# Cosine attention into a gated MLP on one core: scores in threes over three PSUM banks, norms by batch statistics and Newton steps, the last tile in three pieces

## The chip, the cores and the metric

The kernel runs on one core of a Trainium2 chip. The metric is the device time of one execution in microseconds (us); the times of before are the median of 4 runs. TensorE is called PE here, VectorE DVE, ScalarE ACT, GpSimd POOL, and SyncE SP, as in the profile.

## What is computed

8 batches, 12 heads, 448 positions, 64 elements a head, in float32; then an MLP from 768 to 2048 and back.

```python
q_n = q / (np.linalg.norm(q, axis=-1, keepdims=True) + 1e-06)
k_n = k / (np.linalg.norm(k, axis=-1, keepdims=True) + 1e-06)
scores = np.matmul(q_n, k_n.transpose(0, 1, 3, 2)) / tau
scores = scores - np.max(scores, axis=-1, keepdims=True)
attn = np.exp(scores)
attn = attn / (np.sum(attn, axis=-1, keepdims=True) + 1e-09)
x = np.matmul(attn, v)          # (B, H, S, D) -> (B * S, H * D)
h = x @ w_in
g = h * np.cos(h)
out = g @ w_out
```

## The kernel before

**Stages.** The work is cut into 48 pairs of heads (g = 0 to 47, six to a batch, PB = 6) and 16 units of three pairs (u, UP = 3). A unit is loaded in float32 (`load`, line 647 on, q and k; `load_v`), and normed: `square` (L689 on ACT, L691 on DVE, L693 on POOL), `reduce` (L700, DVE: a sum over 64 elements), `rnorm` (L708 and L711, ACT: ln, then exp of -0.5 ln, which is 1/norm), and `scale` (L719, DVE or POOL), which writes q and k as bf16 into `qks`. `transposes` (L734 by DMA from pair BYPE = 9 on, L745 on PE before) makes `qkT`. `scores` (L762) are four chunks a pair, each two matmuls on 64 rows that run side by side, into one of two banks SC0 and SC1; L767 is the exp that reads a chunk and writes PX. `attend` (L785) multiplies PX by v in the AV bank, L794 and L795 divide by the sum that a column of ones gave, and the result goes to xT by DMA (L801) or, for the pairs in XPE, by PE through the AV bank (L809, called XP) and a DVE copy (L813).

When a batch's six pairs are there, `m1` (L826) multiplies by w_in in eight groups over the banks AV, SC0 and SC1 in turn; L840 is ACT's cosine, L842 DVE's product, written to gT. ACT loads a table ahead of the cosines and another behind them (L618). `m2_emit` (L877) multiplies gT by w_out: a tile of 128 rows in two halves of 384 columns, 16 matmuls each, in the banks PO and PO2; DVE copies a half (L884) and SP sends the tile (L895), the last tile half by half (L891, SP and ACT).

**Order.** A planner sets it. Each operation has an engine, its reads and writes, a cost and a latest time; `play` places operations one by one, `arrange` tries several margins and keeps the plan whose rehearsal is shortest, and `emit` writes each engine's instructions in the order of the plan, with the semaphore waits that the reads and writes need. So every engine's order is fixed in the program. PE's operations come in two streams: A (scores, attend, M1, transposes) in groups of which the first three are looked at, and B (M2), of which only the first that is left is looked at (`fill[0]`) when A has nothing that is ready in time. In the first batch (`free`) the order of A is looser. Where PE would stand still in the head, `emit` puts in fillers, products of zeros (line 919, tile zt).

Loads of q, k, v go out on SP (the q of unit 0 on ACT), the weights on POOL with a cast to bf16: w_in in two halves (W1, L908), w_out in four (W2, L914). W1's first half waits until v of unit 0 has landed. A unit has its buffer by its number's last bit, so unit 2 is loaded into unit 0's, pair by pair, once unit 0's scales have read it.

**The steady part.** `pair(g)` gives the order: two chunks of scores, attend of the pair before, then two chunks. Between those PE does M2 of the batch before. After the first pair of a batch comes M1 of the batch before.

The functions that the diff touches:

## Time and profile before

| | |
|---|---|
| median of 4 runs | 433.74 us (433.16 to 434.6) |
| profiled execution | 432.82 us |
| its span, first to last instruction | 430.9 us |
| granted TensorE clock | 1.000 |
| PE busy | 417.8 us (97%), 13.7 of it fillers |
| ACT, DVE, POOL busy | 264.5, 212.9, 192.7 us |
| M1 of the first batch starts | 36.40 us |
| last matmul's row, start and length | 424.77, 2.76 us |

The page's second part shows the span in 40 slices, each digit the busy share in tenths. Groups of instructions are told by line, engine, operation, out<-in with shapes, count, busy time, mean, and the idle time just before them with what ended it. A timeline has the start, the length, engine, line and tiles of instructions in order, like ones merged with their count; in square brackets stands the idle time before one and what released it. PE's matmuls are pipelined: the distance of two starts tells what PE spends, the mean length is longer.

### The profile page before, as it was taken

What the parts mean: (1) busy time and instruction counts of PE and PEld (TensorE: products, weight loads), DVE (VectorE), ACT (ScalarE), POOL (GpSimd) and SP (SyncE); (2) the same over time, 40 slices, a digit from 0 to 9 for tenths busy, and PEclk for the clock granted to TensorE, in tenths of its full rate; (3) what the DMA queues carried; (4) which work ended last, traced back from release to release, by engine and by line L of the source; (5) the groups of instructions that cost most, each with busy time, mean ns of one, the idle gap of its engine ahead of it and who ended that gap; (6) DMA issues with size and microseconds to landing.
All of it is one profiled execution on the core that took longest, in us unless ns stands there. A gap on an engine that the chain in (4) does not pass through costs nothing.

```text
span 430.9 us, 8767 instructions
## 1 busy us (share of the span) xinstructions
PE 417.8 (97%) x3756; PEld 225.8 (52%) x3756; DVE 212.9 (49%) x297; ACT 264.5 (61%) x319; POOL 192.7 (45%) x118
## 2 busy tenths in 40 slices
PE   7889989999999999999999999999999999999996
PEld 2455545545555555555555545555555545555663
DVE  5776646464636366524853375425853343344221
ACT  3887386974777647874677638774777547734000
POOL 3995167923776556922496057913496000000000
PEclk9999999999999999999999999999999999999999
DMA  8999999898189596649757692649447102200322
GB/s 235 262 242 215 240 261 175 143 263 192 34 193 237 112 278 164 124 102 237 185 113 122 166 275 58 113 128 265 127 110 131 49 0 59 59 2 2 102 79 77
DMA packets 94631, 63.87 MB, mean 148 GB/s; under 512 B 55040, under 2 KB 89600, under 8 KB 94592
## 3 DMA queue, kind: packets, MB, share of 16 engines
q1 hardware_dynamic: 90064, 56.16, 55.3%
q0 software_dynamic: 3680, 6.29, 7.9%
q10 hardware_dynamic: 848, 0.86, 0.7%
q8 instruction: 30, 0.49, 0.5%
q14 instruction: 9, 0.07, 0.1%
HBM read 45.61 MB, written 11.01 MB: 131 GB/s over the span
## 4 chain that ended last, share of the span: by engine, by line
PE 83%; ACT 6%; issue 4%; DMA 3%; POOL 2%; DVE 2%; SPq 0%; POOLq 0%; ACTq 0%
PE PO L877 31%; PE SC L826 16%; PE AV L785 11%; PE AV L826 10%; PE SC L762 10%; ACT PX L767 5%; DMA raw<-in_q_dram 3%; PE SC L877 2%; POOL sq L693 1%; PE AV L877 1%; PE AV L809 1%; DVE gT L842 1%; PE PO L745 0%; POOL va L667 0%; DVE n L700 0%
## 5 line engine op out<-in xcount | busy, mean ns | idle before, releaser
L767 ACT ACTIVATE PX<-SC 112x896 bf16<-112x896 f32 x192 | 165.0, 914 | 43.8 <-PE SC L762 43.3
L877 PE MATMUL PO<-W,gT 128*128 128x384 bf16 x816 | 148.6, 326 | 0.0
L693 POOL TENSOR_TENSOR sq<-raw 112x1024 bf16<-112x1024 f32 x42 | 79.3, 1905 | 98.5 <-DMA raw<-in_q_dram 95.1
L877 PEld LDWEIGHTS PO<-W,gT 128*128 128x128 bf16 x816 | 73.0, 97 | 56.8 <-issue 13.1
L719 POOL TENSOR_TENSOR qks<-raw,rn 112x1024 bf16<-112x1024 f32 x47 | 88.4, 1902 | 29.6 <-ACT rn L711 29.4
L826 PE MATMUL SC<-xT,W 128*128 128x448 bf16 x480 | 95.5, 352 | 0.4 <-ACT PX L767 0.4
L842 DVE TENSOR_TENSOR gT<-SC,cosb 128x896 bf16<-128x896 f32 x40 | 43.5, 1091 | 55.1 <-ACT cosb L840 54.8
L840 ACT ACTIVATE cosb<-SC,cst 128x896 f32<-128x896 f32 x40 | 40.2, 1007 | 48.6 <-PE SC L826 46.1
L826 PEld LDWEIGHTS SC<-xT,W 128*128 128x128 bf16 x480 | 46.6, 98 | 43.2 <-issue 0.8
L700 DVE TENSOR_REDUCE n<-sq 112x16 f32<-112x1024 bf16 (+1 forms) x49 | 58.1, 1192 | 14.0 <-POOL sq L693 9.3
L826 PE MATMUL AV<-xT,W 128*128 128x448 bf16 x288 | 58.7, 352 | 1.1 <-DVE gT L842 0.5
L762 PE MATMUL SC<-qkT 64*128 64x448 bf16 x384 | 55.4, 355 | 4.4 <-ACT PX L767 2.2
L785 PEld LDWEIGHTS AV<-va,PX 112*128 112x128 bf16 x1536 | 49.4, 97 | 15.7 <-issue 11.3
L785 PE MATMUL AV<-va,PX 112*128 112x65 bf16 x1536 | 54.8, 193 | 1.1 <-ACT PX L767 1.1
L884 DVE COPY osb<-PO 128x384 f32<-128x384 f32 x51 | 28.2, 553 | 39.0 <-PE PO L877 39.0
L840 ACT ACTIVATE cosb<-AV,cst 128x896 f32<-128x896 f32 x24 | 24.2, 1007 | 32.6 <-PE AV L826 32.5
L794 DVE RECIPROCAL rcp<-AV 112x8 f32<-112x8 f32 x48 | 10.0, 207 | 66.9 <-PE AV L785 66.9
L826 PEld LDWEIGHTS AV<-xT,W 128*128 128x128 bf16 x288 | 27.5, 98 | 28.8 <-issue 3.9
L842 DVE TENSOR_TENSOR gT<-AV,cosb 128x896 bf16<-128x896 f32 x24 | 26.2, 1090 | 18.7 <-ACT cosb L840 18.6
L795 DVE TENSOR_TENSOR xs<-AV,rcp 112x512 bf16<-112x512 f32 x48 | 33.2, 692 | 2.0
L762 PEld LDWEIGHTS SC<-qkT 64*128 64x128 bf16 x384 | 13.2, 93 | 36.9 <-ACT PX L767 17.4
L667 POOL CAST va<-vin 112x1536 bf16<-112x1536 f32 x14 | 20.5, 1465 | 9.1 <-DMA vin<-in_v_dram 6.2
(34 smaller groups left out, 122.0 us busy)
## 6 DMA issues: line engine op xcount, KB each, us to landing
vin<-in_v_dram SPq DMA_DIRECT2D x16, 672.0 KB, 9.9
raw<-in_k_dram SPq DMA_DIRECT2D x12, 672.0 KB, 8.1
raw<-in_q_dram SPq DMA_DIRECT2D x12, 672.0 KB, 10.1
W<-in_moe_w_in_dram POOLq DMA_DIRECT2D x2, 1536.0 KB, 14.6
W<-in_moe_w_out_dram POOLq DMA_DIRECT2D x4, 768.0 KB, 21.3
raw<-in_k_dram SPq DMA_DIRECT2D x12, 224.0 KB, 6.9
out_dram<-osb SPq DMA_DIRECT2D x7, 336.0 KB, 2.8
out_dram<-osb SPq DMA_DIRECT2D x8, 288.0 KB, 2.7
```

Source lines behind the costliest of these rows:

```text
L693: pool(lambda e, x=x, y=y: e.tensor_tensor(y, x, x, ALU.mult), src_, dst, 0.1 + n * 1.78e-3, label="sq%d.%d" % (u, p))
L700: dve(lambda e, w=w: e.tensor_reduce(out=n2v[i][:, 2 * p : 2 * p + 2, w], in_=sqv[p][:, :, w, :], axis=mybir.AxisListType.X, op=ALU.add), ...
L719: f = lambda e, s0=s0, s1=s1: e.tensor_tensor(qksv[i][:, p, s0:s1, :, :].rearrange("p s h d -> p h s d"), rawv[i][:, h, s0:s1, :], bass.AP ...
L762: t = e.matmul(SCv[z][:, a, 0:S], qkT[k].ap()[r, NP * c : NP * c + 128], qkT[k].ap()[r, S : 2 * S], start=True, stop=True)
L767: act(lambda e: e.activation(PXv[j][:, c, 0 : 2 * S].rearrange("p (a s) -> p a s", a=2), SCv[z][0:NP, :, 0:S], ACT.Exp, scale=1.0 / TAU), ...
L785: t = e.matmul(AVv[:, a, DV * x : DV * x + n], PXv[j][:, c, k : k + 128], vav[i][:, NJ * (2 * p + a) + c, 0:n], start=(c == 0), stop=(c == ...
L795: dve(lambda e: e.tensor_tensor(xsv[y].rearrange("p x h d -> p h x d"), AXv[:, :, :, 0:D], bass.AP(rcp[y], 0, [[NS, NP], [NJ, 2], [1, NJ], ...
L826: t = e.matmul(ph[:, a, 0:S], W1v[:, c, 128 * n : 128 * n + 128], xTv[b % 2][:, c, :], start=(c == 0), stop=(c == NKC - 1))
L840: act(lambda e, ph=ph, cz=cz: e.activation(cosv[cz], ph[:, :, 0:S], ACT.Sin, bias=cst.ap()[:, 0:1], scale=1.0), names(gi) + ["cst0"], [("c ...
L842: dve(lambda e, ph=ph, cz=cz, gi=gi: e.tensor_tensor(gTv[:, 2 * gi : 2 * gi + 2, S * (b % 2) : S * (b % 2) + S], ph[:, :, 0:S], cosv[cz], ...
L877: r = e.matmul(po[:, 0:HW], gTv[:, y, col : col + 128], W2v[:, y, HW * hf : HW * hf + HW], start=(y == 0), stop=(y == NF - 1))
L884: dve(lambda e, po=po, o=o, hf=hf: e.tensor_copy(osb[o].ap()[:, HW * hf : HW * hf + HW], po[:, 0:HW]), keys, [("osb", o, hf)], HW, label=" ...
```

## The change

The diff has these parts.

- Units 0.0, 0.1 (ACT squares the means) and 1.0 (POOL does) and all of unit 2 get their sums of squares from `moments`: bn_stats on DVE, 16 instructions of 64 elements to a pair, each leaving count, mean and count times variance of the even and the odd elements; the means are squared and scaled, and a reduce adds up four numbers of each.
- Unit 2's 1/norm comes from `rnorm`'s new branch: a first guess by integer arithmetic on the bits, and three Newton steps, two instructions on DVE and twelve on POOL, for pair 0 and once more for pairs 1 and 2 (N2).
- W1 no longer waits for v of unit 0, and stands on POOL behind the square of pair 2; W2 stands behind the scale of unit 1's last pair.
- From pair 12 on (G3) scores go over three banks, AV, SC0 and SC1, three chunks to a visit, so that three pairs take four visits; M1 (`project`) comes after the second visit of a batch.
- Pairs up to 11 are transposed on PE (BYPE = 12), those from 8 on in the AV bank; unit 2's transposes come after M1 of batch 0. XP uses the banks of M2 instead of AV, from the second batch's last pair on.
- M2: SPREAD of a batch's halves are given after its M1, the rest but KEEP after the last XP of the next batch; the planner looks at the first nine of stream B, if they belong to another half than the first.
- The copy of v on DVE and attend in the first batch come in smaller pieces.
- The last tile has three pieces of 384, 256 and 128 columns.
- The planner's trials and some costs are other numbers.

```diff
 PLAN = {
-    "sq": ["AD", "A", "P", "P", "P", "P"],
+    "sq": ["BA", "BA", "P", "BP", "P", "P"],
     "scale": ["DD", "P", "P", "P", "P", "P"],
 }
...
-    TRIALS = [(m, h, k) for m in ((0.0, 1.0), (0.3, 1.1), (0.8, 1.1)) for h in (0.1, 0.2) for k in (0.05, 0.2)]
+    TRIALS = [(m, h, k, p) for m in ((0.3, 1.1), (0.7, 1.1)) for h in (0.2, 0.32) for k in (0.4, 0.5) for p in (0.15, 0.25)]
...
-            if fill and left[fill[0].idx] == 0:
-                o = fill[0]
-                t = max(free["PE"], ready_at[o.idx])
+            o = None
+            for x in fill[:9]:
+                if left[x.idx] == 0 and (x is fill[0] or x.group != fill[0].group):
+                    y = max(free["PE"], ready_at[x.idx])
+                    if o is None or y < t - 0.15:
+                        o, t = x, y
+            if o is not None:
...
-    BYPE = 9
+    BYPE = 12
...
+    GATE = "T12"
+    BEHIND = "sq0.2"
+    NEWTON, STEPS, STEPSON = (2,), 3, "P"
+    BN, BNU = 0.128, (2,)
+    BU = "BP"
+    N2 = ((0, 1), (1, 3))
+    CUT = 640
+    LASTW = "scale1.2"
+    G3 = 12
+    KEEP = (0, 1, 0, 1, 0, 1, 0)
+    SPREAD = (5, 6, 6, 6, 6, 6, 6)
+    AT, AT1 = 1, 1
...
+    def moments(u, p, how):
         i = u % 2
...
+            def stats(e, t=t):
+                for a in range(2):
+                    for z in range(NJ * t, NJ * t + NJ):
+                        r = e.bn_stats(tuples[:, a, z, :], rawv[i][:, 2 * p + a, z, :])
+                return r
...
+            small(lambda e: e.tensor_scalar(m, m, 1e-12, None, ALU.add), km, km, False)
+            small(lambda e: e.tensor_scalar(y.bitcast(I32), m.bitcast(I32), -0.5, 1597463007.0, ALU.mult, ALU.add), km, ky, False)
+            for x in range(STEPS):
+                small(lambda e: e.tensor_tensor(t, y, m, ALU.mult), km + ky, kt)
+                small(lambda e: e.tensor_tensor(t, t, y, ALU.mult), kt + ky, kt)
+                small(lambda e: e.tensor_scalar(t, t, -0.5, 1.5, ALU.mult, ALU.add), kt, kt, STEPSON == "P")
+                small(lambda e: e.tensor_tensor(y, t, y, ALU.mult), kt + ky, ky)
+            return
...
+        if g >= PB + UP - 1:
+            views, keys = (AVt, AVt), ("AV", "AV")
...
-        j, k, z = g % 2, g % UH, (c + 1) % 2
+        j, k, q = g % 2, g % UH, NJ * g + c
+        name, bank = PHs[1 + (c + 1) % 2 if g < G3 else q % 3]
...
+            cuts = (0, HW, CUT, DM) if t == B * S // 128 - 1 else (0, HW, DM)
...
+    def visit(g, n):
+        q = NJ * g + 3 * n
+        for x in range(q, q + 3):
+            scores(x // NJ, x % NJ)
...
     load_w1(0)
-    after(P.ops[-1], find("load v u0"))
     load_w1(1)
...
+    P.order_only(find(BEHIND0), find("W1.0"))
+    P.order_only(find(BEHIND), find("W1.1"))
...
+    for g in range(G3, NG, 3):
+        for n in range(4):
+            if n < 3:
+                ahead(g + n)
+            grouped(visit, g, n)
+            if n < 3 and g + n > PB:
+                attend(g + n - 1)
+            if n == 0:
+                values(g)
+            if g % PB == 0 and g > PB and n == (AT if g > 2 * PB else AT1):
+                project(g // PB - 1, g)
```

## The prediction

> **What bounds the kernel now.** I read the page's engine rows first, then the groups of TensorE (PE) instructions, then PE's timeline, and ACT's and POOL's only where PE stands still.
>
> ```profile
> span 430.9 us, 8767 instructions
> ...
> PE 417.8 (97%) x3756; PEld 225.8 (52%) x3756; DVE 212.9 (49%) x297; ACT 264.5 (61%) x319; POOL 192.7 (45%) x118
> ...
> PE   7889989999999999999999999999999999999996
> ```
>
> PE is busy in 97% of the span, at full granted clock throughout. So a saving has to come from PE's own time: work that is no work, changes of mode between kinds of matmul, stalls, and the two ends. Not all of the 97% is work. The next lines are groups of PE instructions (busy us, mean ns, idle before them):
>
> ```profile
> L919 PE MATMUL PO<-zt 128*128 128x448 bf16 x48 | 13.7, 404 | 1.6 <-DVE zt L918 1.6
> L762 PE MATMUL SC<-qkT 64*128 64x448 bf16 x384 | 55.4, 355 | 4.4 <-ACT PX L767 2.2 <-DVE gT L842 0.6 <-DVE qkT L753 0.5
> ```
>
> The first is the filler (a product of zeros that the planner puts into gaps): 48 matmuls that only count as busy. The second are the scores, the only matmuls on 64 rows.
>
> In the steady part (start us, length, engine, line, tiles, count) the distance of the starts is what PE spends:
>
> ```profile
> 175.50 0.81 PE L877 MATMUL PO<-W,gT 128*128 128x384 bf16 x4
> 176.25 0.55 PE L762 MATMUL SC<-qkT 64*128 64x448 bf16 x4
> 176.73 2.12 PE L877 MATMUL PO<-W,gT 128*128 128x384 bf16 x12
> 178.79 0.55 PE L762 MATMUL SC<-qkT 64*128 64x448 bf16 x4
> ```
>
> Twelve M2 matmuls alone take 12 x 0.1625 = 1.95 us, but from 176.73 to the scores at 178.79 go 2.06: 0.10 to enter the scores' mode. Four score matmuls run two by two, so 2 x 0.19 = 0.38, but 176.25 to 176.73 is 0.48: 0.10 to leave it. So a visit to the scores costs 0.19 to 0.20 besides its work. A pair of heads has two visits; a batch 12.
>
> Where PE stands or fills, outside the first 36 us:
>
> ```profile
> 56.79 2.12 PE L877 MATMUL PO<-W,gT 128*128 128x384 bf16 x12
> 58.75 0.54 PE L919 MATMUL PO<-zt 128*128 128x448 bf16 x2
> 60.07 0.36 PE L762 MATMUL SC<-qkT 64*128 64x448 bf16 x2 [0.78 <-ACT PX L767]
> 60.37 0.36 PE L919 MATMUL PO<-zt 128*128 128x448 bf16 x1
> ...
> 89.25 0.55 PE L919 MATMUL PO<-zt 128*128 128x448 bf16 x2
> 90.17 4.70 PE L826 MATMUL SC<-xT,W 128*128 128x448 bf16 x24 [0.39 <-ACT PX L767]
> ...
> 108.69 0.36 PE L762 MATMUL SC<-qkT 64*128 64x448 bf16 x2
> 109.64 0.36 PE L762 MATMUL SC<-qkT 64*128 64x448 bf16 x2 [0.59 <-DVE gT L842]
> ```
>
> From 58.75 to 61.98 are 3.2 us in which only three pairs of scores run. At 89.25 0.9 go by before M1 of the second batch, and at 108.69 some 0.6 to 0.7 after it. From 110 us to the last matmul nearly nothing of this kind is left: summed over the starts, about 4 us in 317.
>
> The head (M1 of batch 0 starts at 36.40) is ACT's and POOL's:
>
> ```profile
> 11.46 3.76 POOL L719 TENSOR_TENSOR qks<-raw,rn 112x1024 bf16<-112x1024 f32 x2
> 15.19 3.73 POOL L693 TENSOR_TENSOR sq<-raw 112x1024 bf16<-112x1024 f32 x2
> 15.68 3.34 ACT L767 ACTIVATE PX<-SC 112x896 bf16<-112x896 f32 x4 [1.53 <-PE SC L762]
> ```
>
> ACT runs from the first exp at 9.92 to the end of the 24th at 35.37, 25.4 us: 24 x 0.83 = 20.0 of exps, five pairs of ln and rn at 0.54 = 2.7, and 2.7 of waiting, 1.53 of it before pair 1. POOL has a square (1.9) and a scale (1.9) for most pairs, 3.8, more than ACT's four exps (3.3).
>
> **The change, part by part.** Sums are against the profiled execution: 432.82 us, that is the span of 430.9 and 1.9 around it; the median of the runs, 433.74, lies 0.92 above it.
>
> 1. *Visits of three chunks over three banks* (G3 = 12, pairs 12 to 47). 36 pairs made 72 visits and make 48. 24 x 0.19 = **-4.6**. The same matmuls and exps stand as before. What is added is a wait: every visit's first chunk goes to the AV bank and waits there until attend's reciprocal and xs have read it, and behind it on PE stand the other two chunks and M2. By rows of the head: score start to exp 0.40 (9.52 to 9.92), exp 0.91, AV after it 0.05 (35.37 to 35.42), AV start to reciprocal 1.18 (35.42 to 36.60), to xs 0.24, xs 0.69, 0.06 to PE: 3.53. Three pairs have four visits, one without an attend (1.42): 12.0. PE has three periods (AV of one pair at 112.06, of the third after it at 126.20: 14.14) less 0.38 = 13.8 for them. So it fits, with 1.8 to spare, and M2 lies over it.
>
> 2. *M2 chosen from nine entries, and kept back* (fill[:9], SPREAD, KEEP). At 58.75 PE had done 12 of the 16 matmuls of one half tile and the planner could only look at the next; the other half tile has its own bank and 12 more that are ready: 1.95 us of work in place of filler. Of the 2.3 us of filler time I take **-1.7**; bounds 0 and -2.3. At 89 to 110 the held-back halves cover M1's entry and exit: losses 0.9 + 0.7, I take **-1.1**; bounds 0 and -1.6.
>
> 3. *Transposes of pairs 9 to 11 on PE* (BYPE 12) instead of by DMA: 3 x 8 x 0.049 = **+1.2** on PE, and three DVE copies of 0.62 beside other work. They use the AV bank between attends; transpose, copy and latency are 0.39 + 0.28 + 0.62, in a period with room for it. Transposes of pairs 6 and 7 move out of M1(0) to behind it, before scores that wait for the table load and the first exp at 59.10 anyway: nothing, or 0.8 if they are not hidden. XP goes to the M2 banks: no count changes.
>
> 4. *The last tile in 384, 256 and 128 columns.* The last copy is 128 columns: 0.556 - 256/960 = 0.289, **-0.27**. PE: 16 matmuls more with their 2.5 ns, +0.04. The landing, from these rows (the last copy and issue; issues with KB and us to landing):
>
> ```profile
> 427.57 0.56 DVE L884 COPY osb<-PO 128x384 f32<-128x384 f32 x1 [1.97 <-PE PO L877]
> 428.17 0.38 ACTq L891 DMA_DIRECT2D out_dram<-osb  x1
> ```
> ```profile
> out_dram<-osb ACTq DMA_DIRECT2D x1, 168.0 KB, 2.3
> out_dram<-osb SPq DMA_DIRECT2D x2, 24.0 KB, 1.7
> ```
>
> 56 KB lies between 1.7 and 2.3, in proportion 1.8. Between no gain and -0.6 I take -0.3: the rows of a piece are shorter (512 bytes). Together **-0.5**. The middle piece is issued 0.8 us ahead on the same queues and lands earlier.
>
> The Trainium skill speaks against this cut twice. TensorEngine Tiling (Array Packing), Instruction Overhead, gives each matmul some 60 cycles of overhead; 16 more would be 0.4 us at 2.4 GHz. The trace doesn't show that for rows of short matmuls: 32 of 65 columns from 174.52 to 175.50, 31 ns each. DMA: Bandwidth & Descriptors, Anatomy of one DMA, gives 2.0 us fixed and bytes/436 GB/s, so 0.26 less for 56 KB than for 168; an estimate from its fit for another queue, and close to what I take.
>
> 5. *The head.* Added: units 0.0, 0.1, 1.0 and all of 2 take statistics on DVE, 16 instructions of 64 elements for each. No row shows one. Below: the 59 ns of a one-element memset; above: 207 ns of a small reciprocal. The reduces (680 ns for 512, 1213 for 1024) give 0.067 us for 64 elements plus some 0.06 to 0.11 of fixed cost: I take 0.15, 2.4 us for 16. For pair 0: loads land at 4.30 and 4.66, 4.3 + 2.4 = 6.7, the small square on ACT and the small reduce 0.6, so ln at 7.3 where it was at 6.72: first exp +0.6 (bounds -0.9 and +1.6). Against it: the square of unit 1.0 leaves POOL (-1.9, two small instructions of some 0.2 instead), ACT's square of 0.1 goes, and what stood behind on POOL (scale 1.0 at 19.54, 1.1 at 23.25, 1.2 at 27.51) comes 1.5 or more earlier, so that part of ACT's 2.7 of waiting goes; I take -1.1. DVE gets 2 x 1.2 more in 26 us, in which it was busy 19.9. Net **-0.5** at M1's start, bounds -2.5 and +2.0.
>  Unit 2's norms: twelve small POOL instructions and two on DVE, twice. Between the 105 ns of a memset and 0.35 I take 0.25 (iota, 217): 2 x 3.0 us. They replace two squares (3.8) on POOL, one on ACT (1.08), ln and rn (0.58) between the last exp and the table load. The cover: POOL is idle 4.6 us before 39.38 and 11.4 before 56.43, and pair 6 is wanted at 56.3. So nothing on the path. DMAs: unit 2's loads were issued at 8.7 to 15.6 already and W1's first packets flow at about 15, 5 us after POOL issued; W1's halves landed at 27.4 and 37.3, wanted at 36.4 and about 46, so their order has some 9 us of cover. W1 no longer waits for v's landing, but stands behind a square that ends at 10.36, and was issued at 10.34.
>
> Sum: -4.6 - 1.7 - 1.1 + 1.2 - 0.5 - 0.5 = **-7.2**. Profiled execution 425.6, median **426.5**.
>
> **The rivals.**
> - *The AV bank holds the visits up but no more than it saves* (0.16): part 1 gives nothing, 426.5 + 4.6 = 431.1. For it: one bank now has three users. Against: 1.8 us to spare per three pairs.
> - *The head is DVE's* (0.12): statistics at 207 ns, first exp +1.6 and the copies behind them late; M1 2.0 later instead of 0.5 earlier: 426.5 + 2.5 = 429.0. For it: 0.15 is worked out, not measured.
> - *The part that gives the change its name does nothing* (0.05): loads and norms of unit 2 were in time before. M1 starts at 36.4 as now: 427.0. The gain is then that of the visits and the filler.
> - *Slower* (0.15): the visit's exp of the AV bank stands behind one exp of the visit before (0.83), and once in three pairs the reciprocal behind an output copy (0.56). Per three pairs 3 x 0.83 + 0.56 - 1.8 = 1.25 of PE standing still, twelve times: 426.5 + 15 = 441.5. PE's order is fixed, so M2 behind the visit can't step in. It makes the kernel slower than before from about 0.8 us of such waiting per attended visit: (1.8 + 7.2/12)/3.
>
> **How the numbers follow.** My forecast has 0.52, with its own range 423 to 429.5 from the bounds of parts 2 to 5. A measurement here tells 0.2% (0.9 us) from no change. Faster: 0.52 + 0.05 + 0.15 of the first rival + 0.10 of the second = 0.82; same 0.03, the upper ends of these two; slower 0.15. The range goes from 423.0 (a head at -2.5 with most filler and stalls gone) to 433.0, and leaves out the slower case and some 0.03 below.
>
> **What would show it.** Scores in rows of six matmuls from pair 12 on, 48 visits, and PE waits on xs or on exps at most a few tenths in sum. Less filler near 58 and 89. Transposes of qks on PE: 96 instead of 72. Statistics of 16 in 2.0 to 2.8 us; first exp at 10.2 to 10.8; M1(0) at 35 to 36.5; from last matmul to the end 3.0 instead of 3.5. Wrong would be a wait of PE for DVE's xs at each visit, or M1(0) after 37.5.

## The result and the profile after

| | before | changed |
|---|---|---|
| median, all runs | 434.61 us (78 runs) | 432.91 us (54 runs) |
| ratio to before, 95% interval | 1 | 0.9961 [0.995, 0.9973] |
| profiled execution, its span | 432.82, 430.9 | 434.89, 433.1 |
| second profile of the same kernel, its span | none | 432.38, 430.6 |

The change gains 0.4%, some 1.7 us, where 7.2 was forecast. The profiled execution of before lies 1.8 below its median, the first of the changed kernel 2.0 above; so below the changed kernel is told by both its profiles.

The page after, engine rows, PE's slices and granted clock:

```profile
span 433.1 us, 8988 instructions
...
PE 420.2 (97%) x3798; PEld 230.6 (53%) x3798; DVE 222.7 (51%) x403; ACT 260.3 (60%) x316; POOL 194.4 (45%) x147
...
PE   8899998999899999999999999999999999999997
...
PEclk9899999999999999999999999999999999999999
```

The busy share is 97% again; it doesn't tell the two kernels apart. What does is an account of PE by start distances: each instruction is charged its work (M2 0.1625, M1 0.189, two score matmuls side by side 0.187, AV 0.029, a transpose 0.049 us), up to 0.097 at each step into or out of scores is a mode change, fillers are counted whole, and the rest is waiting. M1(b) is M1 of batch b. From one M1 to the next (before; changed, first and second profile; us):

| stretch | mode changes | filler | waiting |
|---|---|---|---|
| head to M1(0) (at 36.40; 37.45, 36.22) | 2.60; 3.67, 3.66 | 13.70; 15.82, 14.95 | 5.02; 2.85, 2.50 |
| M1(0) to M1(1) | 2.97; 3.45, 3.45 | 3.27; 0, 0 | 1.31; 4.07, 3.36 |
| M1(1) to M1(2) | 2.66; 1.52, 1.52 | 0; 0, 0 | 1.56; 3.84, 2.58 |
| M1(2) to M1(7), five stretches | 10.66; 7.26, 7.26 | 0; 0, 0 | 3.82; 6.94, 7.64 |
| M1(7) to the end | 0; 0, 0 | 0; 0, 0 | 3.62; 2.62, 2.62 |

So the mode changes behind M1(1) fell from 13.3 to 8.8, and the fillers behind M1(0) went; waiting took most of both.

In the steady part of the changed kernel (timeline of PE, then of ACT, as in the prediction) one sees the visits of three and the first kind of new wait:

```profile
166.89 0.36 PE L845 MATMUL AV<-qkT 64*128 64x448 bf16 x2
167.09 0.54 PE L845 MATMUL SC<-qkT 64*128 64x448 bf16 x4
167.56 1.48 PE L966 MATMUL PO<-W,gT 128*128 128x384 bf16 x8
169.07 1.14 PE L868 MATMUL AV<-va,PX 112*128 112x65 bf16 x32
170.05 1.46 PE L966 MATMUL PO<-W,gT 128*128 128x384 bf16 x8
```
```profile
167.29 0.92 ACT L850 ACTIVATE PX<-AV 112x896 bf16<-112x896 f32 x1
168.11 1.72 ACT L850 ACTIVATE PX<-SC 112x896 bf16<-112x896 f32 x2
```

Six score matmuls stand in one visit, 166.89 to 167.56. Eight M2 matmuls are 1.30, but attend starts 1.51 behind them: PE waits 0.20 for the second of the three exps, which ends near 169. Two such waits and three of 0.04 come in every batch of the steady part.

The second kind stands near 67 and 109. Near 67 PE waits for a scale on POOL, which stands behind a cast of v, which waits for a load (POOL, then PE):

```profile
65.26 1.47 POOL L705 CAST va<-vin 112x1536 bf16<-112x1536 f32 x1 [1.82 <-DMA vin<-in_v_dram]
66.68 5.62 POOL L795 TENSOR_TENSOR qks<-raw,rn 112x1024 bf16<-112x1024 f32 x3
```
```profile
68.73 0.55 PE L827 MATMUL AV<-ident,qks 112*128 112x112 bf16 x8 [1.59 <-POOL qks L795]
```

Near 109 (POOL, DVE, then PE):

```profile
106.07 5.59 POOL L727 TENSOR_TENSOR sq<-raw 112x1024 bf16<-112x1024 f32 x3 [5.78 <-DMA raw<-in_q_dram]
```
```profile
107.99 1.22 DVE L756 TENSOR_REDUCE n<-sq 112x16 f32<-112x1024 bf16 x1 [1.21 <-POOL sq L727]
109.13 1.08 DVE L933 TENSOR_TENSOR gT<-AV,cosb 128x896 bf16<-128x896 f32 x1
```
```profile
110.36 2.43 PE L917 MATMUL AV<-xT,W 128*128 128x448 bf16 x12 [1.26 <-DVE gT L933]
```

Read from the bottom: M1 waits for a product gT on DVE, which stands behind a reduce, which waits for a square on POOL, which waits for a load. Each engine has its order, so one late load holds PE. Before had the same chain at 105.35 to 109.64, 0.7 earlier; it cost PE 0.6. Its square on POOL:

```profile
105.35 5.60 POOL L693 TENSOR_TENSOR sq<-raw 112x1024 bf16<-112x1024 f32 x3 [7.21 <-DMA raw<-in_q_dram]
```

In the head (DVE, then POOL):

```profile
4.90 3.14 DVE L736 BATCH_NORM_STATS2 st<-raw 112x6 f32<-112x64 f32 x24 [3.34 <-DMA raw<-in_q_dram]
7.96 0.20 DVE L747 TENSOR_REDUCE n<-st 112x16 f32<-112x64 f32 x1
8.07 1.10 DVE L736 BATCH_NORM_STATS2 st<-raw 112x6 f32<-112x64 f32 x8
9.09 2.76 DVE L795 TENSOR_TENSOR qks<-raw,rn 112x512 bf16<-112x512 f32 x2
```
```profile
8.81 1.89 POOL L727 TENSOR_TENSOR sq<-raw 112x1024 bf16<-112x1024 f32 x1 [7.32 <-DMA raw<-in_q_dram]
10.65 1.89 POOL L999 DMA_DIRECT2D W<-in_moe_w_in_dram  x2
13.60 3.75 POOL L795 TENSOR_TENSOR qks<-raw,rn 112x1024 bf16<-112x1024 f32 x2 [1.06 <-ACT rn L787]
```

24 statistics take 3.14, 0.131 each, so 16 take 2.1. But eight of pair 1 stand ahead of pair 0's reduce, and the two halves of pair 0's scale take 2.76 where before they took 1.29, beside a square on POOL that started first: the first half takes 2.16 and ends 0.55 behind that square, the second takes 0.68. Pair 1's reduce stands behind this scale on DVE, so POOL waits 1.06 for pair 1's 1/norm and scales it from 13.60 (before 11.46). First exp at 13.50 (before 9.92). Both halves of W1 are issued by 12.5; before, the second went at 25.1. Unit 2's loads, forecast to be ahead, landed from 26.9 to 41.3 (before 22.3 to 30.2).

The tail (the last copy; issues with KB and us to landing):

```profile
430.68 0.29 DVE L975 COPY osb<-SC 128x128 f32<-128x128 f32 x1 [0.47 <-PE SC L966]
```
```profile
out_dram<-osb ACTq DMA_DIRECT2D x1, 112.0 KB, 1.9
out_dram<-osb ACTq DMA_DIRECT2D x1, 56.0 KB, 1.6
```

From the last matmul's start to the end: 2.67 (before 3.72).

### The profile page after: what moved, and what is told of

It is laid out like the page before. It is cut to its first block, busy times and chain, and to the rows that moved or that the text cites. A ratio compares the mean times of both kernels' runs of the same rounds, so it can differ in the third digit from the quotient of the medians.

```text
span 433.1 us, 8988 instructions
## 1 busy us (share of the span) xinstructions
PE 420.2 (97%) x3798; PEld 230.6 (53%) x3798; DVE 222.7 (51%) x403; ACT 260.3 (60%) x316; POOL 194.4 (45%) x147
## 4 chain that ended last, share of the span: by engine, by line
PE 75%; POOL 7%; DMA 6%; ACT 5%; DVE 5%; issue 1%; SPq 1%; DVEq 0%; ACTq 0%
PE PO L966 24%; PE SC L917 19%; PE AV L917 11%; PE AV L868 9%; DMA raw<-in_q_dram 6%; PE SC L845 5%; POOL qks L795 3%; ACT PX L850 3%; POOL sq L727 3%; PE AV L845 2%; DVE st L736 1%; PE SC L966 1%; DVE gT L933 1%; PE AV L966 1%; ACT cosb L931 1%
## 5 line engine op out<-in xcount | busy, mean ns | idle before, releaser
L966 PE MATMUL PO<-W,gT 128*128 128x384 bf16 x832 | 152.4, 327 | 0.7 <-DVE osb L975 0.6
L850 ACT ACTIVATE PX<-SC 112x896 bf16<-112x896 f32 x144 | 123.3, 916 | 5.0 <-PE SC L845 4.7
L966 PEld LDWEIGHTS PO<-W,gT 128*128 128x128 bf16 x832 | 74.1, 98 | 63.2 <-issue 18.6
L727 POOL TENSOR_TENSOR sq<-raw 112x1024 bf16<-112x1024 f32 x39 | 73.1, 1893 | 75.5 <-DMA raw<-in_q_dram 71.3
L850 ACT ACTIVATE PX<-AV 112x896 bf16<-112x896 f32 x48 | 44.0, 917 | 47.6 <-PE AV L845 47.6
L756 DVE TENSOR_REDUCE n<-sq 112x16 f32<-112x1024 bf16 x42 | 50.8, 1213 | 13.7 <-POOL sq L727 12.6
L868 PE MATMUL AV<-va,PX 112*128 112x65 bf16 x1536 | 56.0, 193 | 0.8 <-ACT PX L850 0.2
L845 PE MATMUL SC<-qkT 64*128 64x448 bf16 x288 | 42.5, 354 | 2.3 <-ACT PX L850 0.8
L878 DVE RECIPROCAL rcp<-AV 112x8 f32<-112x8 f32 x48 | 9.9, 207 | 62.9 <-PE AV L868 62.9
## 6 DMA issues: line engine op xcount, KB each, us to landing
W<-in_moe_w_in_dram POOLq DMA_DIRECT2D x2, 1536.0 KB, 22.3
```

What stands on the lines that cost most here:

```text
L727: pool(lambda e, x=x, y=y: e.tensor_tensor(y, x, x, ALU.mult), src_, dst, 0.1 + n * 1.78e-3, label=name)
L756: dve(lambda e, o=o, hs=hs: e.tensor_reduce(out=n2v[i][:, o, :], in_=sqv[p][:, hs[0] : hs[-1] + 1, :, :], axis=mybir.AxisListType.X, op=AL ...
L845: t = e.matmul(bank[:, a, 0:S], qkT[k].ap()[r, NP * c : NP * c + 128], qkT[k].ap()[r, S : 2 * S], start=True, stop=True)
L850: act(lambda e: e.activation(PXv[j][:, c, 0 : 2 * S].rearrange("p (a s) -> p a s", a=2), bank[0:NP, :, 0:S], ACT.Exp, scale=1.0 / TAU), [n ...
L868: t = e.matmul(AVv[:, a, DV * x : DV * x + n], PXv[j][:, c, k : k + 128], vav[i][:, NJ * (2 * p + a) + c, 0:n], start=(c == 0), stop=(c == ...
L966: r = e.matmul(po[:, 0 : w1 - w0], gTv[:, y, col : col + 128], W2v[:, y, w0:w1], start=(y == 0), stop=(y == NF - 1))
```

## The experiments

Each edit makes the planner lay out the whole order anew, unless said otherwise, so that stalls shift too (the two kernels that differ in the last tile alone keep the order up to that tile, on every engine); the account by stretches shows what came from where. Ratios are to runs of before on the same chip, with 95% intervals. A stall is a wait of PE.

| kernel | median us | ratio | profiled span | M1(0) at |
|---|---|---|---|---|
| changed, again | 431.71 | 0.9965 [0.9937, 0.9993] | 430.6 | 36.22 |
| square behind scale, order kept | 433.18 | 0.999 [0.9966, 1.0013] | 430.5 | 38.25 |
| square behind scale, planned | 432.75 | 0.9975 [0.995, 0.9999] | 429.1 | 37.34 |
| unit 0 by squares | 432.34 | 0.9962 [0.9941, 0.9982] | 430.5 | 38.67 |
| visits undone | 433.13 | 0.9977 [0.9956, 0.9998] | 431.2 | 36.65 |
| attend behind the fourth visit | 432.82 | 0.9969 [0.9946, 0.9992] | 433.3 | 36.72 |
| M2 by the first entry | 433.17 | 0.9983 [0.9957, 1.0009] | 433.6 | 36.56 |
| transposes by DMA | 438.09 | 1.009 [1.006, 1.0121] | 439.5 | 36.45 |
| last tile in halves | 433.02 | 0.9967 [0.994, 0.9995] | 431.3 | 36.98 |
| before, last tile in three | 432.67 | 0.997 [0.9947, 0.9993] | 431.0 | 36.86 |
| W1 late | 431.70 | 0.9934 [0.9911, 0.9956] | 431.4 | 36.98 |
| unit 2 by ln | 435.30 | 1.0038 [1.0006, 1.007] | 433.2 | 36.70 |
| W1 late, unit 2 by ln | 436.09 | 1.0033 [1.0009, 1.0056] | 434.9 | 37.22 |
| W1 late, transposes by DMA | 435.61 | 1.0038 [1.0007, 1.0068] | 434.0 | 37.80 |
| W1 late, visits undone | 433.96 | 0.9993 [0.9967, 1.0018] | 433.9 | 36.57 |
| three edits | 432.92 | 0.9974 [0.9945, 1.0004] | 430.9 | 38.55 |
| W1 late, fourth visit, pair 16 | 432.34 | 0.9961 [0.9937, 0.9985] | 432.4 | 36.56 |
| the same, square behind scale | 434.98 | 1.0006 [0.9981, 1.0032] | 435.8 | 39.16 |

**The changed kernel again.**

> The changed kernel once more, unchanged, for a second profile. In the first, M1 of batch 0 began at 37.45, PE waited 1.6 us at 68.7 for unit 3's scale on POOL, and 1.3 at 110.4 for DVE. If these two waits belong to the program, they stand again, each over 1 us, and the span is near 433. If they came from loads that landed late in that one execution, they are under 0.5 here and the span is 429 to 431; the waits of 0.2 us ahead of AV, two to a batch, stand in both cases.

The waits stand again: 1.26 at 65.6 for POOL, 1.55 at 106.8 for gT, and 0.20 twice a batch. A third profile of the same order, that with the last tile in halves below, has 1.15 at 66.3 and 1.29 at 107.1. They belong to the kernel, not to one execution.

**The head: does DVE's scale or POOL's chain set M1(0)?** Two ways of putting POOL's square behind the scale (a wait added to the finished order, and one known to the planner), and pairs 0 and 1 without statistics:

```diff
+    after(find("sq0.2"), find("scale0.0"))
```
```diff
-    "sq": ["BA", "BA", "P", "BP", "P", "P"],
+    "sq": ["AD", "A", "P", "BP", "P", "P"],
```

> The changed kernel with one wait more: POOL's square of unit 0's pair 2 starts behind DVE's scale of pair 0, and every other place in every engine's order stays. Theory: DVE's two scale halves took 2.76 us instead of 1.3 because POOL's square had started 0.3 us before and the two share a way to memory; then they take 1.3 to 1.5, the first scores come 1.2 to 1.5 earlier (near 11.3 for 12.8), POOL's scale of pair 1 about 0.6 later, and M1 of batch 0 comes 0 to 1 earlier: time 0 to 1 us less. Rival (the scale is long for another reason, such as its operands): the halves stay at 1.4 each and the time rises by up to 1 us, since POOL is later.

> As a1 (POOL's square of pair 2 behind DVE's scale of pair 0), but known to the planner, which orders everything anew. In a1 the scale took 1.28 and first scores came at 11.5, yet M1 of batch 0 came at 38.25, 0.8 to 2 later, since POOL's scale of pair 1 stood behind a later square and W1's issues. Theory now: POOL's chain is the head's path; the planner can put the square behind the scale of pair 1, so M1 comes at 35.5 to 37 and the time is 0 to 1 us under the changed kernel. Rival: the square is simply late, M1 near 38, 1 us more.

> The changed kernel with the first two pairs normed as before (squares on ACT and DVE, then reduces); the planner orders anew. The changed kernel's first scores came at 12.0 to 12.8 in two profiles, before's at 9.5. Theory: the statistics on DVE, with the next pair's eight put in ahead of the small reduce, and the scale behind POOL's square cost the head 2 to 3 us, which it makes up only in part; without them first scores near 9.6 and M1 of batch 0 at 34.5 to 35.8 instead of 36.2 to 37.4: 0.5 to 1.5 us less than the changed kernel (ratio 0.993 to 0.995). Rival: POOL's chain (square, two issues of W1, scale after scale) sets M1's start whatever pair 0 does; then M1 stays at 36 to 37 and the time within 0.5.

The scale fell to 1.28 and 1.29:

```profile
8.80 1.29 DVE L795 TENSOR_TENSOR qks<-raw,rn 112x512 bf16<-112x512 f32 x2
```

(DVE with the square replanned.) But M1(0) came no earlier, at 38.25 and 37.34 (changed 37.45 and 36.22), with a wait of 2.4 for POOL's scale of pair 1 in the first. With squares for unit 0 the first scores stood at 9.75 (changed 12.77 and 12.02), and M1(0) at 38.67. So the first scores, 3 us late, don't set M1(0); POOL's chain of squares and scales mostly does: in these three profiles and the two of the changed kernel the last exp of the first batch ends 7.6 to 8.2 us behind POOL's last scale of unit 1. With squares for unit 0 one more wait comes in behind it, of DVE for a load of unit 2 ahead of a copy to xT (DVE, then PE):

```profile
37.12 1.11 DVE L736 BATCH_NORM_STATS2 st<-raw 112x6 f32<-112x64 f32 x8 [0.92 <-DMA raw<-in_q_dram]
```
```profile
38.67 2.05 PE L917 MATMUL SC<-xT,W 128*128 128x448 bf16 x10 [1.08 <-DVE rcp L878]
```

What the long scale costs the end isn't shown. Moving the square takes POOL's wait of 1.06 (1.05 in the second profile) ahead of pair 1's scale away, but puts the square in its place: that scale starts at 14.34 and 13.19, where it stood at 13.60 and 12.85.

The first of the three has the order of the changed kernel on every engine. Its M1(0) is 2.03 later than in the changed kernel's second profile, its M1(2) only 0.75 (143.31 and 142.56): the waits near 67 and 107, 1.26 and 1.55 there, are 0.31 and nothing here. Between these two profiles, most of what PE had gained at M1(0) it spent waiting for loads later.

**The visits.** Undone (two chunks over two banks for all pairs); attend of a round's second pair behind the fourth visit:

```diff
-    for g in range(G3, NG, 3):
...
+    for g in range(G3, NG):
+        ahead(g)
+        grouped(both, g, 0)
+        attend(g - 1)
```
```diff
-            if n < 3 and g + n > PB:
-                attend(g + n - 1)
+            if n != 2 and g + n > PB:
+                attend(g + (0, 1, 2, 2)[n] - 1)
```

> The changed kernel with the visits undone: from pair 12 on two chunks of scores to a visit over the two banks SC0 and SC1, M1 at the same place (behind chunk 5 of three pairs and the attend that follows). If the visits bring what was predicted, it is 4.6 us slower than the changed kernel (ratio to before 1.006 to 1.007). If the waits ahead of AV (2 x 0.2 and a few of 0.04 a batch) and the like take it back, as the account of the first profile says (3.4 us fewer for switches, 3.1 us more of other losses over batches 3 to 7), it is within 1 us of the changed kernel (ratio 0.995 to 0.999).

> The changed kernel with one attend of each three pairs moved: that of the second pair stands behind the fourth visit instead of the third, so that it no longer follows at once on the exp of its own last chunk, which is the second chunk of the third visit. Theory: the waits of 0.2 us of PE ahead of AV (12 to 24 in all) come from that; they go, 2 to 3 us less than the changed kernel. Rival (they are the price of the AV bank, whichever attend it is): they move to the other visit and the time stays within 0.7 us.

Undone, a batch without a stall has 2.29 of mode changes and 1.04 of waiting; with visits 1.53 and 1.29. So visits save 0.5 a batch, not 0.76. The medians put their worth at 0.5 us in all (0.9977 to 0.9965), within the error; most of the 2.5 to 3 that five or six batches should give was eaten by larger stalls near 67, 107 and 174. With attend behind the fourth visit the 0.20 waits are gone (waiting 1.02 a batch), but two stalls of 2.3 came, at 107 and at 143, and the time stood.

**M2's choice and the transposes.**

```diff
-                for x in fill[:9]:
+                for x in fill[:1]:
```
```diff
-    BYPE = 12
+    BYPE = 9
```

> The changed kernel with the planner looking at the first entry of M2's stream alone, as before. Theory: the filler of 2 to 3 us between M1 of batch 0 and the first exps comes back; 1.5 to 3 us more than the changed kernel (ratio 0.999 to 1.003). Rival: what the second half tile filled is lost again a few us later, at the transposes that wait for POOL; then within 0.7 of the changed kernel.

> The changed kernel with pairs 9 to 11 transposed by DMA, as before (BYPE 9). Theory: 1.2 us of PE's work go, and the wait of 1.1 to 1.6 us for POOL's scale at 66 to 69, where the transposes of pair 9 stand in PE's order ahead of scores and M2 that could run; 1 to 2.5 us less (ratio 0.991 to 0.994). Rival: the scores of pair 9 then wait for the DMA behind the same scale, and the time stays within 0.7.

With one entry no filler came back; PE stalled 2.8 at 106.7 for gT instead of 1.5. So it isn't the choice that took the filler away. That the order around it did (unit 2's transposes stand behind M1 now) fits the profiles of unit 2 by ln below, where these transposes come later and fillers are back, but wasn't tested by itself. With DMA transposes PE stalled 4.6 at 72.0 and 3.5 at 113.2: my expectation fell, and the 1.2 us of transposes on PE are well spent in this order.

**The tail**, taken back alone and put on the kernel before alone:

```diff
-            cuts = (0, HW, CUT, DM) if t == B * S // 128 - 1 else (0, HW, DM)
+            cuts = (0, HW, DM)
```

> The changed kernel with its last tile in two halves again, as before; all else in the same order, but for the first matmuls of the last tile. If the cut of the last tile is worth what the two profiles show at their ends (last matmul to the end 3.56 before, 2.50 changed), this kernel is 0.5 to 1.1 us slower than the changed one, and its stretch from the last matmul's start to the end is 3.4 to 3.6 us again. Rival: the piece of 128 columns only moves the wait to another landing; then the end is within 0.3 us of the changed kernel's.

> The kernel before with one part of the change alone: its last tile in pieces of 384, 256 and 128 columns. Theory: the tail is the one part whose gain nothing takes back, so 0.5 to 1.1 us less than before, with 2.4 to 2.8 us from the last matmul's start to the end in place of 3.56. Rival: nothing within what can be measured (0.2%), since the landing of the last piece is the same whatever its size.

From the last matmul's start to the end: 3.73 in halves (changed 2.67); 2.71 for before in three pieces (3.72 in halves). 1.07 and 1.01 us: shown. The medians agree in sign. Before with this part alone stands at 0.997, the whole change at 0.9961, so by the medians the tail could be most of what the change gains; the intervals meet.

**Is the early W1 the cause of the stalls near 67 and 107?** W1's second half as late as before, and unit 2 by squares, ln and exp:

```diff
-    P.order_only(find(BEHIND), find("W1.1"))
+    P.order_only(find("scale1.1"), find("W1.1"))
```
```diff
-    NEWTON, STEPS, STEPSON = (2,), 3, "P"
-    BN, BNU = 0.128, (2,)
+    NEWTON, STEPS, STEPSON = (), 3, "P"
+    BN, BNU = 0.128, ()
```

> The changed kernel with the second half of W1 issued only behind the scale of unit 1's second pair, as it stood before, and the order made anew for that. Theory (the waits near 66 and 107 us are the end of a chain: W1's second half, issued at 11.7 instead of 25.1 us, shares the DMA engines with unit 2's loads, which land at 27 to 41 instead of 22 to 30; unit 2's norms on POOL end at 57.6 instead of 45.0, unit 3's square and scale come late, PE's transposes of pair 9 wait, and DVE's reduce, late behind POOL, holds gT up): unit 2's loads land by 33, its norms end on POOL by 51, PE waits under 0.5 us near 66 and under 0.7 near 107, and the kernel is 1 to 2.5 us faster than the changed one. Rival (the norms' own 24 POOL instructions or the order made for PE set the waits, the loads don't): the landings move and the waits stay, within 0.7 us of the changed kernel.

> The changed kernel with unit 2 normed as before the change (squares on ACT and POOL, sums on DVE, ln and exp on ACT), the order made anew for that; units 0.0, 0.1 and 1.0 keep their statistics. Theory (the change's named part was not needed, because unit 2's norms were in time before, and it loads POOL): within 0.8 us of the changed kernel, with POOL's wait ahead of pair 9's transposes no longer. Rival (the norms by POOL's steps do save ACT and so the first batch): 1 to 3 us slower, with ACT's waits near 36 to 58 us back.

With the late W1 unit 2 landed by 36.3 (38.8 to 41.3 changed), its scales on POOL ended at 53.1 (56.4 to 57.6), and the stalls near 67 and 107 went. But what PE had waited for there came no earlier (POOL with the late W1):

```profile
64.95 1.47 POOL L705 CAST va<-vin 112x1536 bf16<-112x1536 f32 x1 [1.13 <-DMA vin<-in_v_dram]
66.38 5.62 POOL L795 TENSOR_TENSOR qks<-raw,rn 112x1024 bf16<-112x1024 f32 x3
```

The scale starts at 66.38 (64.94 and 66.68 in the changed kernel's two profiles), behind a cast whose load of v landed at 64.90 (63.46 and 65.20); PE's new order has M2 and scores up to 68.8 and doesn't stand. Near 107 q's load landed at 105.97 (104.17 and 106.00); M1 had begun 14.4 before that instead of 13.1 and 13.0, and its product on DVE went ahead of the reduce. So the order made anew took the two stalls away, and my theory of unit 2's late loads isn't shown. New ones came, 0.9 at 62.9 (for a cast of v) and at 138.7, and 1.4 at 158.1, the last of the same form, M1 waiting for gT. The ratio, 0.9934, is the lowest of all; its interval meets that of the changed kernel, so whether it is faster stays open.

Unit 2 by ln was 3 us slower than the changed kernel, against my theory. ACT and PE there:

```profile
56.61 1.28 ACT L640 ACT_TABLE_LOAD   x1
57.91 0.31 ACT L784 ACTIVATE lnn<-n,cst 112x16 f32<-112x16 f32 x1
```
```profile
59.44 0.82 PE L966 MATMUL PO<-W,gT 128*128 128x384 bf16 x4 [1.99 <-DMA W<-in_moe_w_out_dram]
60.10 0.73 PE L1010 MATMUL PO<-zt 128*128 128x448 bf16 x3
```

ACT takes ln only behind the cosines and the table load, so unit 2's transposes come at 62.9; with Newton steps they begin at 54.9 and 56.1 (second and first profile) and, with scores and M2 that is ready, fill PE until the last quarter of W2 has landed (58.0 and 59.8). Without them PE has only M2 and runs into that landing.

**Are Newton's steps and the PE transposes needed only because the early W1 makes things late?** The late W1 with ln, with DMA transposes, and with visits undone:

> The changed kernel with W1's second half behind the scale of unit 1's second pair and unit 2 normed as before the change (squares, and ln and exp on ACT), order made anew. With unit 2 by ln alone the time rose by some 3 us: ACT's ln and exp stood behind the cosines and the table load, at 57.9, and PE ran out of other work near 57. Theory (unit 2's Newton steps mend a lateness that the early W1 makes): with the loads early again ln and exp come before the cosines, at 36 to 45, and the time is within 0.8 us of the kernel with the late W1 alone. Rival (the Newton steps are worth their time by themselves, by taking ln out of ACT's order): 2 to 4 us slower than that kernel, with ln behind the table load again.

> The changed kernel with W1's second half behind the scale of unit 1's second pair and pairs 9 to 11 transposed by DMA as before (BYPE 9), order made anew. With BYPE 9 alone PE stood 4.5 us at 72.0 for the transposed pair and 3.4 us at 113. Theory (those waits are the same late chain: unit 3's scale comes late because unit 2's loads and norms do): with the loads early both waits fall under 1.5 us and the kernel is within 1 us of the kernel with the late W1 alone, or faster by up to 1.2. Rival (the transposes by DMA take too long for the order of this kernel wherever the loads stand): 3 to 6 us slower than the kernel with the late W1 alone, and the waits stay over 2.5 us each.

> The changed kernel with W1's second half behind the scale of unit 1's second pair, and scores by pairs of chunks over two banks as before the change (no visits of three), order made anew. It measures the visits a second time, on another order of the first two batches. Theory (visits save 0.76 us a batch of mode changes and give 0.2 to 0.3 back in waits ahead of attend): a clean batch is 0.4 to 0.6 us longer, and the time 0.5 to 3 us above the kernel with the late W1 alone. Rival (visits give nothing or cost, since the AV bank holds them up in the batches before the steady part): no slower than that kernel.

No, twice: both are 1.0% slower than the late W1 alone (by their ratios). With ln the sums were there at 39.8, and the table load had already gone at 35.1, so ln waited for 58.4 all the same; before, it stood at 38.69, ahead of the table load at 39.32. Whether the changed order with that one change does without Newton's steps wasn't tried. With DMA transposes the stall at 72 went, that at 107.5 stayed (2.7). Undoing the visits cost 0.6%, some 2.5 us, of which a stall of 1.9 at 73.0, and the half clock behind it, are a part.

**Can the visits' saving be kept?** Three edits together (W1 late, square behind scale, attend behind the fourth visit); then without the square's edit but with pair 16 turned by PE; then with both:

```diff
-    XPE = set(range(PB)) | set(range(PB - 1, NG, PB))
+    XPE = set(range(PB)) | set(range(PB - 1, NG, PB)) | {16}
...
-        if g >= 2 * PB - 1:
+        if g >= 2 * PB - 1 and g != 16:
             m2_emit(max(0, len(m2_queue) - KEEP[g // PB - 1]))
```

> The changed kernel with three edits together: W1's second half behind the scale of unit 1's second pair, POOL's square of pair 2 behind its scale of pair 0, and the attend of the second pair of a round behind the fourth visit instead of behind the third; order made anew. Theory (what took the visits' savings back are PE's 0.2 us waits ahead of attend and the stalls near 66 and 107, each of which one of these edits takes away): less than each edit alone, 1 to 3 us below the changed kernel (429 to 431.5), a clean batch 0.25 us shorter, no stall of PE over 1 us between the first M1 and the last batch. Rival (stalls of PE only move to another place with each new order, as with the edits alone): within 1 us of the changed kernel, with a stall of over 1 us at a new place.

> The changed kernel with W1's second half behind the scale of unit 1's second pair, the attend of the second pair of a round behind the fourth visit, and pair 16's result turned by PE and a DVE copy instead of by DMA (in the order with three edits, M1 of the third batch waited 2.1 us for that DMA at 139.7, and the granted clock then fell for some 3.5 us, at a price of 1.7). Theory (with the waits ahead of attend and that stall gone, the visits' savings stay): no stall over 1 us from 100 us on, and 428 to 430.5 us. Rival (the stall goes to the next late transfer or product): within 1 us of the changed kernel (431 to 433.5) with a stall of over 1 us at another place.

> The same, with POOL's square of pair 2 behind its scale of pair 0 as well. Theory of the shared path of DVE and POOL: scale 0.0 takes 1.3 instead of 2.1 to 2.8 us and the first scores start 0.5 to 1.1 us earlier, but M1 of the first batch starts no earlier, since POOL's chain of squares and scales sets it: M1(0) 0 to 1.5 us later than without this edit, and the time 0 to 1.5 us longer. Rival (first scores set M1's start): M1(0) and the time 0.5 to 1 us earlier.

In the second a batch without a stall has 1.52 of mode changes and 0.64 to 0.77 of waiting: 2.2 in all, where before had 3.0. There the saving of 0.76 a batch is whole. But each of the three met one large stall: 2.3 at 139.7 for the DMA of xT, then 3.8 at 156.2 and at 157.8. In the second kernel (PE, then POOL):

```profile
160.22 3.56 PE L917 MATMUL AV<-xT,W 128*128 128x448 bf16 x12 [3.65 <-DVE gT L933]
```
```profile
153.80 5.59 POOL L727 TENSOR_TENSOR sq<-raw 112x1024 bf16<-112x1024 f32 x3 [6.88 <-DMA raw<-in_q_dram]
```

It is the chain of 106 to 110 once more, one batch later. The rival held: the stall goes to another late load. With the square's edit as well M1(0) came at 39.16, 2.6 later than without it, and the time rose by 0.45%: more than I had expected of that edit. None of the versions beat the changed kernel by more than the measurement tells.

## Why the prediction was wrong

The sign, the range and the tail's mechanism held; the size didn't. Against before's profile, first and second profile of the changed kernel:

| step | forecast | measured |
|---|---|---|
| 1, mode changes behind M1(1) | -4.6 | -4.5, -4.5 |
| 1, waits in the five later stretches | 0 | +3.1, +3.8 |
| first batch, mode changes behind M1(0) | 0 | +0.5, +0.5 |
| 2, filler and waits, M1(0) to M1(2) | -2.8 | +1.8, -0.2 |
| 3, transposes | +1.2 | +1.2, +1.2 |
| 4, tail | -0.5 | -1.0, -1.0 |
| 5, M1(0) | -0.5 | +1.05, -0.2 |
| sum | -7.2 | +2.1, -0.4 |

The spans differ by +2.2 and -0.3.

- **Part 1 failed at "it fits, with 1.8 to spare".** The bank's cycle does fit; scores in the AV bank hardly waited. But I checked the cycle's length and not the order inside it: attend needs the second exp of its visit, and PE reaches attend 0.2 before that exp ends. Without stalls a batch lost 3.01 before and loses 2.81; with the attend moved 2.55; in the best order 2.2.
- **Part 2 failed.** The fillers went (3.3 to 0), as forecast; the places they filled were a real lack of ready work, and waits of the same size stand in the same two stretches: 4.07 and 3.84 of waiting where 1.31 and 1.56 had been. I took away what was idle without asking what released PE at its end. The row at 109.64, a wait for gT, was on the page, and its chain through DVE and POOL to a load could have been followed.
- **The norms of unit 2 were "nothing on the path"**, with "some 9 us of cover" for W1. The loads landed up to 11 us later than before (the late W1 takes back 2.5 to 5 of that), and unit 2's scales end at 56.4 to 57.6 instead of 45.0. I had priced W1's landing and not what its packets do to others. That this lateness reached PE isn't shown: ahead of unit 3's scales, for which PE's transposes at 67 wait, POOL stands 0.68 and 1.82 for loads of v. What the early W1 costs stays open.
- **Part 3** was right on PE. The other side was put at nothing: by DMA these transposes cost 4.5 to 5.6 us more here (1.0038 against 0.9934 with the late W1, 1.009 against 0.9961 without).
- **Part 4** was right in kind and half its size: copy -0.27 as worked out, landing 1.6 instead of 2.3 (-0.7, not -0.3).
- **Part 5** had the price of the statistics nearly right (2.1 for 16, forecast 2.4). It had the first exp wrong (13.5, forecast 10.2 to 10.8), since the order put eight more statistics and a long scale ahead. M1(0), forecast 0.5 earlier, came 1.05 later and 0.2 earlier, inside the bounds.
- **Rivals.** "AV bank holds the visits up" (431.1) came nearest, with other waits than named. "The named part does nothing" fell for this order: without Newton's steps 435.3.

What stays open: where the 1.7 us of the medians stand in the profiles, when the second profile's span gains 0.3. The profile of before is one of its faster executions, so the measured column sets the changed kernel against a fast one. Before with the last tile in three has before's order up to that tile, and so gives a second look at it: M1(0) 0.46 later, and stalls of 0.62 at 74.6 and 0.78 at 160.6 that the first profile lacks. With the tail's 1.0 added its span would be 432.0, and the second profile of the changed kernel lies 1.4 below that, near the medians.

## What to carry to other kernels

Where every engine's order is fixed, a saving on the bounding engine is kept only if what releases it comes earlier too; price a removed switch or filler together with the next releaser, followed back through each engine to its load. Where loads set the waits, an earlier PE only waits longer: between two profiles of one order, 2.0 us at M1(0) were 0.75 two batches on. Check not only that a buffer's cycle fits its period, but that each waiter in it is reached after its operand is ready. A transfer that is issued earlier is a change to every transfer behind it.

## What the runs showed of the hardware

**The granted clock halves behind a stall, on a fixed grid.** Windows of the kernel with three edits (length, busy times of PE, PEld, DVE, ACT and POOL, clock, DMA share, GB/s):

```profile
128.00:138.00 10.00, 10.00 (x122) 5.67 (x119) 6.97 (x11) 7.63 (x12) 5.60 (x3) 1.00 0.79 178
139.70:142.00 2.30, 0.17 (x6) 0.07 (x3) 0.90 (x2) 1.84 (x2) 2.30 (x2) 1.00 0.97 235
142.00:146.00 4.00, 4.00 (x13) 1.72 (x14) 0.00 (x0) 0.00 (x0) 4.00 (x3) 0.58 0.42 78
```

PE stood 2.3 us; 0.7 after it began again each matmul took twice its time for 3.4 us, a further 1.6 us lost. Outside the head, of eleven stalls of 1.9 us or more in these profiles eight were followed by this (0.9 to 2.5 us lost each), three weren't, and none of those up to 1.76. Length alone doesn't decide. The stretches at 0.50 last 3.41 us (twice 6.83), and in the eight profiles with one in the work and one at the end their starts lie a whole number of 3.413 us apart, 81 to 123 of them: the clock changes on a fixed grid. Cut into steps of that grid, every step with more than 2.06 us without a matmul (transposes not counted as one) was followed by half clock, and none with less than 2.05, but for one that ran at half clock itself. That transposes don't count is fitted to these steps, not tested. The three stalls without a drop were split by the grid; the longest, 3.4 us with DMA transposes, in two steps:

```profile
111.92:115.33 3.41, 1.64 (x9) 0.65 (x7) 0.77 (x1) 1.48 (x2) 2.70 (x2) 1.00 0.18 47
115.33:118.74 3.41, 1.82 (x10) 1.00 (x11) 3.41 (x4) 0.00 (x0) 2.90 (x2) 1.00 0.02 5
```

In the head three profiles have such a stretch, from 11.8, 13.1 (the changed kernel's first profile) and 16.5 us. The Trainium skill, TensorE: Matmul & The Clock Gate, Part 1: The HAM clock gate, says that the clock halves after an idle window of about 3.4 us and is given back after a busy one; the length at half clock agrees, but here a step that was idle for 2.1 of its 3.4 us was enough. It makes a stall of 2 us and more dearer than it looks.

**DVE's two-input product beside POOL.** Half of the scale took 0.69 us by itself. Where it started inside a square on POOL it took 2.16 and 1.47 (two profiles), and ended 0.55 and 0.56 behind that square in both; in before the scale was first, and the square took 2.32 instead of 1.89. The Trainium skill, SBUF — State Buffer, SBUF: two separate sides, puts this down to a port pair that the one that starts first holds for its whole instruction; the trace agrees. Taking the overlap away brought M1(0) no nearer.

**Small instructions.** bn_stats of 64 elements came every 0.131 us; the Newton steps on POOL took 0.20 to 0.25 each and came every 0.30 to 0.33, 3.6 to 3.9 us for twelve.
